# Sums of batch 2 for a layer norm: five GpSimd additions, tile by tile, in place of four VectorE reductions

## The chip, the cores and the metric

The kernel runs on one core of a Trainium2 chip. The metric is the device time of one execution in microseconds (us). The core has five engines that run side by side, each through its own queue in order: TensorE (PE in the rows; PEld is its weight load), VectorE (DVE), ScalarE (ACT), GpSimd (POOL) and SyncE (SP, which here only issues DMAs). They meet through semaphores: an instruction that needs another engine's result waits, and everything behind it on its own engine waits too.

## The reference

Attention with normed queries and keys, then two MLPs, all in float32. The part around the change is the mean over features in the first MLP's layer norm, which is taken over the attention's output.

```python
q_n, k_n = rmsnorm(q, g_q), rmsnorm(k, g_k)
scores = scale * np.matmul(q_n, k_n.transpose(0, 1, 3, 2))    # 4 batches, 12 heads, 448 x 448
attn = np.exp(scores - np.max(scores, axis=-1, keepdims=True))
attn = attn / (np.sum(attn, axis=-1, keepdims=True) + 1e-09)
x = np.matmul(attn, v)                                        # then to (4, 448, 768)
...
mu = np.mean(x, axis=-1, keepdims=True)
var = np.mean((x - mu) ** 2, axis=-1, keepdims=True)
xn = (x - mu) / np.sqrt(var + 1e-06) * g_ln
x = x + np.maximum(xn @ w_ch1, 0.0) @ w_ch2
...
u = x + (x.transpose(0, 2, 1) @ U @ V).transpose(0, 2, 1)
out = u + np.maximum(u @ w_ch1, 0.0) @ w_ch2
```

## The kernel before

Each batch's activations `x[b]` lie in SBUF as six tiles of 128 features by 448 tokens (`x[b][:, k, :]`, KD = 6). The kernel has two stages: attention (to about 339 us in the profile) and the MLPs, whose order is set by a planner of its own.

In the attention stage the function `attention` runs 48 heads in a software pipeline. Its loop calls generators, one step of each per quarter of a head: `sc` makes scores (`ps`, L491 and L492) and exponentials (`p`, ACT, L494), `mx` makes scores the other way round (`pm`, L455) and their maxima on VectorE (`m`, L456), `t1` and `t2` transpose (`pk`, `pq`, `pt`), `pv` multiplies by the values (`po`, L509), and `norm` copies the result out of PSUM (`u`, L523) and sends it to `x[b]` and, for the sums of the exponentials, to DRAM.

A list `ln` holds side work that advances by one step of its first generator in each quarter of a head. When the twelve heads of batch 2 are through, it holds in this order: `scale` (reads the sums back, inverts them, spreads them over the partitions as tiles `r`, and multiplies the six tiles of `x[2]` by them on VectorE, L564); `ln_stats(2)`; `early`, which narrows the first MLP weights from float64 (integer joins on VectorE, `join` L83 and `sign` L87) and splits them into a high and a low part (a cast on ScalarE, L945, a subtraction on GpSimd, L946, tiles `w0` to `w5`); the first steps of `scale` for batch 3; and `late`, more weights.

`ln_stats` makes the sums over features in two steps. First four reductions on VectorE, one for each 112 tokens, add the six tiles into one 128x448 tile `xs` (L163). Then a matmul with a matrix of 1/768 adds over the partitions (L169, into the PSUM tile `ln`), and ScalarE copies the mean to `mu` (L172). Six subtractions on GpSimd (L184), squares on ScalarE (L187), sums on VectorE (L181) and a second matmul (L192) make the variance.

A scheduler puts the attention stage's instructions in order on each engine, by its own estimates; those wrapped in `pin`, the norm's matmuls and the scalings among them, keep the program's order. The reductions and the GpSimd operations are not pinned.

Of the kernel before, what the change touches and what calls it, by code (L numbers as in the profile page):

```python
# [8 lines left out]
F32 = mybir.dt.float32  # L9
# [5 lines left out]
ALU = mybir.AluOpType  # L15
AX = mybir.AxisListType

B, H, S, D = 4, 12, 448, 64
P = 128
# [28 lines left out]
def build(tc, qkv, gg, g_ln, w1a, w2a, w1b, w2b, u_in, v_in, out):  # L48
    nc = tc.nc
    V, A, PL, PE = nc.vector, nc.scalar, nc.gpsimd, nc.tensor  # L50
    with ExitStack() as es:
# [96 lines left out]
            by(V.scalar_tensor_tensor(t, t, -0.5, a, ALU.mult, ALU.mult))  # L148
            by(V.scalar_tensor_tensor(y if to is None else to, t, 1.5, y, ALU.add, ALU.mult))

        lns, side = {}, {}

        def ln_stats(b, pool=None):
            def lt(n, pool=None):
                if pool:
                    return pool.tile([P, S], F32, tag="lx", name=f"ln{b}_{n}", bufs=4)
                return lpool.tile([P, S], F32, tag="lt", name=f"ln{b}_{n}")

            lag = 2 if pool else 1
            xs = lt("xs")  # L160
            for c in range(NC):
                cs = slice(c * CP, (c + 1) * CP)
                V.tensor_reduce(xs[:, cs], x[b][:, :, cs].rearrange("p k n -> p n k"), AX.X, ALU.add)  # L163
                yield
            yield
            if pool:
                yield
            pm = side["ln"] if pool else bank("mu")
            pin(PE.matmul(pm[:, :S], ones_m, xs, start=True, stop=True))  # L169
            yield  # L170
            mu = lt("mu")
            pin(A.copy(mu, pm[:, :S]))  # L172
            yield
            acc = lt("acc")
            run = pm[:, :S] if pool else acc
            sqs = {}
            gap = 2 * lag
            for n in range(KD + gap):
                k = n - gap
                if k > 0:  # L180
                    pin(V.tensor_tensor(acc if k == KD - 1 else run, run, sqs[k], ALU.add))  # L181
                if n < KD:
                    sqs[n] = acc if n == 0 else lt(f"sq{n}", pool if n != KD - 2 else None)
                    PL.tensor_tensor(sqs[n], x[b][:, n, :], mu, ALU.subtract)  # L184
                k = n - lag
                if 0 <= k < KD:
                    pin(A.activation(sqs[k] if k else run, sqs[k], AF.Square))  # L187
                yield
            for _ in range(lag):
                yield  # L190
            va = pm if pool else bank("var")
            pin(PE.matmul(va[:, :S], ones_m, acc, start=True, stop=True))  # L192
            yield
            y, a, t = acc, va[:, :S], xs if pool else lt("nt")
            pin(V.tensor_scalar(a, a, EPS, None, ALU.add))
            yield
            pin(A.activation(y, a, AF.Ln))
            pin(A.activation(y, y, AF.Exp, scale=-0.5))
            yield
            rsqrt_newton(y, a, t, a if pool and b < 2 else y)  # L200
            yield
            lns[b] = (mu, a if pool and b < 2 else y)
# [23 lines left out]
        def attention(ap, ep, ep2, early, late):  # L226
# [300 lines left out]
                q.dma_start(st["sum", b][h:h + 1, :], u[D:D + 1, :])  # L527
                yield

            def scale(b, q, h0, h1, pool=None):  # L530

                def fold(d):
                    return d[h0:h1].rearrange("h s -> (h s)").rearrange("(p n) -> p n", p=P)

                n = (h1 - h0) * S // P
                s = lpool.tile([P, n], F32, tag="sc", name=f"ss{b}_{h0}", bufs=2)
                q.dma_start(s, fold(st["sum", b]))
                yield
                y = lpool.tile([P, n], F32, tag="sc", name=f"sy{b}_{h0}", bufs=2)
                yield  # L540
                pin(A.activation(y, s, AF.Ln, bias=tiny))
                pin(A.activation(y, y, AF.Exp, scale=-1.0))
                yield
                pin(V.scalar_tensor_tensor(s, s, 1e-9, y, ALU.add, ALU.mult))
                V.tensor_tensor(s, s, y, ALU.mult)
                V.scalar_tensor_tensor(y, y, 2.0, s, ALU.mult, ALU.subtract)
                yield
                d = dpool.tile([H, S], F32, tag="rs", name=f"rs{b}_{h0}")
                q.dma_start(fold(d), y)
                yield  # L550
                ks = range(h0 // 2, h1 // 2)
                rs = {}
                lag = 3 if pool else 2
                for n in range(len(ks) + lag):
                    if n < len(ks):
                        k = ks[n]
                        rs[k] = (f32(pool)[:, n, :] if pool else
                                 lpool.tile([P, S], F32, tag="lt", name=f"r{b}_{k}"))
                        for j in range(2):
                            q.dma_start(rs[k][j * D:(j + 1) * D, :],  # L560
                                        d[2 * k + j:2 * k + j + 1, :].to_broadcast([D, S]))
                    if n >= lag:
                        k = ks[n - lag]
                        pin(V.tensor_tensor(x[b][:, k, :], x[b][:, k, :], rs[k], ALU.mult))  # L564
                    yield
# [9 lines left out]
            for i in range(-3 - T1, NH + 2):  # L575
                def ok(n):
                    return 0 <= n < NH
                if i == -3 - T1:
                    start = first_two()
                    next(start)  # L580
                elif i == -1 - T1:
                    bg.append(start)
                elif i in (1 - T1, 3 - T1):
                    bg.append(pre((i + T1 + 3) // 2))
                if i > 3 - T1 and (i + T1) % 2 == 0 and (i + T1 + 4) // 2 < NP:
                    bg.append(pre((i + T1 + 4) // 2))
                if i % 2:
                    if 0 <= (i + 1) // 2 < NP:
                        bg.append(pre_v((i + 1) // 2))
                tasks = [f(n) for f, n in (ORD(i)) if ok(n)]  # L590
                if i == 4:
                    ln.append(load_uv())
                if i - 2 in (H, 2 * H, 3 * H):
                    b = (i - 2) // H - 1
                    ln.append(scale(b, nc.sync, 0, H, xl[b] if b < 2 else None))
                if i - 2 in (H, 2 * H):
                    ln.append(ln_stats(b, ap))
                    ln.append(ln_apply(b, ap))
                if i - 2 == 3 * H:
                    ln.append(ln_stats(2, ap))  # L600
                    most = scale(B - 1, nc.sync, 0, HL)
                    ln += [early, islice(most, 5), late]
                for c in range(NC):
                    bg = [t for t in bg if next(t, 1) is None]
                    tasks = [t for t in tasks if next(t, 1) is None]
                    if ln and next(ln[0], 1) == 1:
                        ln.pop(0)
                assert not tasks and not bg or i < NH + 1
# [906 lines left out]
```

## Time and profile before

| what | value |
|---|---|
| median of three runs | 1677.04 us (1676.89 to 1685.16) |
| the profiled execution | 1676.77 us |
| its span, from first to last instruction | 1674.5 us |
| around the span | 2.27 us |
| PE busy | 1659.7 us, 99% |
| DVE busy | 1218.4 us, 73% |
| POOL busy | 1087.7 us, 65% |
| ACT busy | 1003.2 us, 60% |

The span is what the profile's rows cover; the execution's own time holds 2.27 us more. Busy shares are means over both stages. The rows below give start times from the span's start, so that an instruction can be found in all views by its start.

### The profile page before, as it was taken

To read this page: it belongs to the slowest core of one execution; us is meant where nothing else is said; L and a number is where in the kernel's file an instruction comes from. 1 tells how busy PE (TensorE), PEld (TensorE's weight loads), DVE (VectorE), ACT (ScalarE), POOL (GpSimd) and SP (SyncE) were. 2 spreads that over 40 slices of the span, in tenths; PEclk is the share of its full clock that TensorE was granted. 3 is DMA by queue.
4 is the path that set the end of the run, shared out by engine and by line. 5 is a ranking of instruction groups with operands and counts; after the bars stand their busy time and mean duration, and the time that the engine had idled before them with its cause. 6 is when DMAs were issued, how large, how long until landed. Compare 5 with 4: busy or idle time off the path is not lost.

```text
span 1674.5 us, 24807 instructions
## 1 busy us (share of the span) xinstructions
PE 1659.7 (99%) x8251; PEld 1442.0 (86%) x8251; DVE 1218.4 (73%) x1941; ACT 1003.2 (60%) x2105; POOL 1087.7 (65%) x963
## 2 busy tenths in 40 slices
PE   8999999999999999999999999999999999999999
PEld 6676666589999999999999999999999999999998
DVE  6878787879887887866767686667667854565665
ACT  6888888767878866554544455444445534454541
POOL 5788767449767787755555587555555655776752
PEclk8999999999999999999999999999999999999999
DMA  3444445776755566544444427565657463443432
GB/s 97 117 100 116 120 117 138 200 223 199 243 173 178 180 212 200 187 141 134 152 133 158 162 83 257 187 219 179 224 192 246 169 207 116 149 151 123 149 125 76
DMA packets 134432, 273.42 MB, mean 163 GB/s; under 512 B 37280, under 2 KB 57664, under 8 KB 134304
## 3 DMA queue, kind: packets, MB, share of 16 engines
q1 hardware_dynamic: 112252, 265.24, 49.8%
q10 hardware_dynamic: 22052, 6.59, 1.7%
q8 instruction: 66, 1.08, 0.3%
q14 instruction: 62, 0.51, 0.1%
HBM read 178.80 MB, written 81.96 MB: 156 GB/s over the span
## 4 chain that ended last, share of the span: by engine, by line
PE 89%; DMA 3%; DVE 3%; issue 2%; ACT 1%; POOL 1%; SPq 0%; POOLq 0%; DVEq 0%; ACTq 0%
PE bank L1120 34%; PE bank L1298 32%; PE bank L1242 6%; PE po L509 4%; PE b L1120 2%; PE b L1242 2%; PE ps L491 2%; PE pm L455 2%; PE ps L492 1%; DVE m L456 1%; DMA raw<-in_qkv 1%; PE t L987 1%; PE xt L977 1%; PE pk L434 1%; PE pq L442 1%
## 5 line engine op out<-in xcount | busy, mean ns | idle before, releaser
L1298 PE MATMUL bank<-h,w 128*128 128x448 f32 x2655 | 586.4, 366 | 0.3 <-DVE h L1112 0.3
L1298 PEld LDWEIGHTS bank<-h,w 128*128 128x128 f32 x2655 | 497.2, 188 | 40.0 <-DVE h L1112 0.6
L1309 DVE TENSOR_TENSOR x<-x,bank 128x448 f32<-128x448 f32 x450 | 275.9, 616 | 192.9 <-PE bank L1298 188.1
L1120 PE MATMUL bank<-xh,w 128*128 128x448 f32 x1158 | 330.4, 367 | 0.0
L794 POOL TENSOR_TENSOR w<-wf,w 128x384 fp32r<-128x384 f32 x201 | 222.6, 1118 | 131.6 <-ACT w L793 131.5
L794 POOL TENSOR_TENSOR w<-s,w 128x384 fp32r<-128x384 f32 x151 | 173.8, 1154 | 155.3 <-ACT w L793 149.9
L1120 PE MATMUL bank<-T,w 128*128 128x448 f32 x1134 | 251.9, 367 | 0.0
L1120 PEld LDWEIGHTS bank<-xh,w 128*128 128x128 f32 x1158 | 216.9, 188 | 18.1 <-issue 0.8
L1120 PEld LDWEIGHTS bank<-T,w 128*128 128x128 f32 x1134 | 211.9, 188 | 16.8
L1120 PE MATMUL bank<-xl,w 128*128 128x448 f32 x579 | 211.7, 366 | 0.0
L793 ACT CAST w<-s 128x384 fp32r<-128x384 f32 x151 | 77.0, 515 | 178.5 <-PE bank L1120 166.0
L793 ACT CAST w<-wf 128x384 fp32r<-128x384 f32 x201 | 101.5, 514 | 101.2 <-PE bank L1120 82.6
L456 DVE TENSOR_REDUCE m<-pm 112x1 f32<-112x448 f32 x192 | 118.5, 619 | 46.4 <-PE pm L455 45.7
L509 PE MATMUL po<-p,vf 112*66 112x448 f32 x328 | 149.8, 539 | 0.1
L83 DVE SCALAR_TENSOR_TENSOR wf<-wf,raw 128x384 uint32<-128x384 uint32 x180 | 134.2, 752 | 10.4 <-ACT raw L71 3.8
L794 POOL TENSOR_TENSOR w<-raw,w 128x384 fp32r<-128x384 f32 x72 | 81.2, 1145 | 57.2 <-ACT w L793 57.1
L1120 PEld LDWEIGHTS bank<-xl,w 128*128 128x128 f32 x579 | 108.8, 188 | 8.7
L79 ACT ACTIVATE wf<-raw 128x384 f32<-128x384 f32 x180 | 99.3, 553 | 20.7 <-DMA raw<-in_w2a 9.5
L494 ACT ACTIVATE p<-ps 112x448 f32<-112x448 f32 x192 | 104.6, 547 | 6.2 <-PE ps L492 3.5
L1112 DVE SCALAR_TENSOR_TENSOR h<-tm,h 128x448 fp32r<-128x448 f32 x103 | 102.2, 992 | 2.8 <-ACT h L1111 2.1
L71 ACT ACTIVATE raw<-raw 128x384 uint32<-128x384 uint8 x180 | 99.9, 558 | 0.0
L1161 DVE TENSOR_TENSOR tm<-tm,bank 128x448 f32<-128x448 f32 x102 | 63.0, 617 | 47.7 <-PE bank L1120 46.8
(283 smaller groups left out, 2989.5 us busy)
## 6 DMA issues: line engine op xcount, KB each, us to landing
wd<-wf SPq DMA_DIRECT2D x94, 384.0 KB
ws<-w SPq DMA_DIRECT2D x84, 384.0 KB
w<-ws SPq DMA_DIRECT2D x84, 384.0 KB
wf<-wd SPq DMA_DIRECT2D x51, 384.0 KB
raw<-wd SPq DMA_DIRECT2D x48, 384.0 KB
raw<-in_w1b SPq DMA_DIRECT2D x48, 384.0 KB
raw<-in_w2b SPq DMA_DIRECT2D x48, 384.0 KB
raw<-in_w2a SPq DMA_DIRECT2D x44, 384.0 KB
```

The costliest lines, as they stand in the source:

```text
L71: A.activation(r[:, :, 0], r.bitcast(U8).rearrange("p n (t q) -> p n t q", t=2)[:, :, 0, 3], AF.Copy, scale=1.0 / 32, bias=-31.0 / 64)
L83: V.scalar_tensor_tensor(f, f, 3, r[:, :, 0], ALU.logical_shift_left, ALU.bitwise_or)
L456: V.tensor_reduce(m[:, c:c + 1], pm[:CP, :S], AX.X, ALU.max)
L494: A.activation(p, pb[:CP, :S], AF.Exp)
L509: PE.matmul(po[:QW, :S], vf[:, j, c, :], ps[c], start=(i == 0), stop=(i == NC - 1))
L793: job(A, 520, lambda: A.copy(form(key)[0], src()), ins, ("hi",) + key, [key])
L794: job(PL, 1100, lambda: PL.tensor_tensor(form(key)[1], src(), f32(form(key)[0]), ALU.subtract), [("hi",) + key], key, rel=rel)
L1112: soon(V, 700, lambda: V.scalar_tensor_tensor(at(*key)[:, 1], src(), 0.0, f32(at(*key)[:, 0]), ALU.max, ALU.subtract), [("hh",) + key], ke ...
L1120: PE.matmul(out[:, :S], wt[:, k, :], xt[:, k, :], start=(first and n == 0), stop=(last and n == 8), skip_group_check=True)
L1242: PE.matmul(at(*to)[:, :S], wt[:, e, :], xt, start=(m in "13" and n == 0), stop=(n == 2), skip_group_check=True)
L1298: PE.matmul(at(*key)[:, :S], wt[:, e % 3, :], t, start=(n == 0), stop=(n == 3 * G - 1))
L1309: V.tensor_tensor(x[b][:, e, :], x[b][:, e, :], at(*key)[:, :S], ALU.add)
```

## The change

For batch 2 alone, `scale` gets `add=True`: after the sixth load of `r` it takes the tile `xs` and adds the scaled tiles into it on GpSimd, five additions of 128x448 (the first joins tiles 0 and 1). `scale` then has one step more. `ln_stats(2)` finds `xs` in `sums` and leaves out the four reductions together with their six steps, so that it begins with the mean's matmul. All work behind it in the list `ln` thus comes five steps sooner. Batches 0, 1 and 3 keep the reductions.

```diff
--- before.py
+++ after.py
@@ -148,7 +148,7 @@
             by(V.scalar_tensor_tensor(t, t, -0.5, a, ALU.mult, ALU.mult))
             by(V.scalar_tensor_tensor(y if to is None else to, t, 1.5, y, ALU.add, ALU.mult))
 
-        lns, side = {}, {}
+        lns, side, sums = {}, {}, {}
 
         def ln_stats(b, pool=None):
             def lt(n, pool=None):
@@ -157,14 +157,17 @@
                 return lpool.tile([P, S], F32, tag="lt", name=f"ln{b}_{n}")
 
             lag = 2 if pool else 1
-            xs = lt("xs")
-            for c in range(NC):
-                cs = slice(c * CP, (c + 1) * CP)
-                V.tensor_reduce(xs[:, cs], x[b][:, :, cs].rearrange("p k n -> p n k"), AX.X, ALU.add)
-                yield
-            yield
-            if pool:
-                yield
+            if b in sums:
+                xs = sums.pop(b)
+            else:
+                xs = lt("xs")
+                for c in range(NC):
+                    cs = slice(c * CP, (c + 1) * CP)
+                    V.tensor_reduce(xs[:, cs], x[b][:, :, cs].rearrange("p k n -> p n k"), AX.X, ALU.add)
+                    yield
+                yield
+                if pool:
+                    yield
             pm = side["ln"] if pool else bank("mu")
             pin(PE.matmul(pm[:, :S], ones_m, xs, start=True, stop=True))
             yield
@@ -527,7 +530,7 @@
                 q.dma_start(st["sum", b][h:h + 1, :], u[D:D + 1, :])
                 yield
 
-            def scale(b, q, h0, h1, pool=None):
+            def scale(b, q, h0, h1, pool=None, add=False):
 
                 def fold(d):
                     return d[h0:h1].rearrange("h s -> (h s)").rearrange("(p n) -> p n", p=P)
@@ -551,7 +554,7 @@
                 ks = range(h0 // 2, h1 // 2)
                 rs = {}
                 lag = 3 if pool else 2
-                for n in range(len(ks) + lag):
+                for n in range(len(ks) + lag + add):
                     if n < len(ks):
                         k = ks[n]
                         rs[k] = (f32(pool)[:, n, :] if pool else
@@ -559,7 +562,12 @@
                         for j in range(2):
                             q.dma_start(rs[k][j * D:(j + 1) * D, :],
                                         d[2 * k + j:2 * k + j + 1, :].to_broadcast([D, S]))
-                    if n >= lag:
+                    if add and n >= len(ks) - 1:
+                        if n == len(ks) - 1:
+                            sums[b] = xs = lpool.tile([P, S], F32, tag="lt", name=f"ln{b}_xs")
+                        for k in (1, 2) if n == len(ks) - 1 else (n - lag - 1,):
+                            PL.tensor_tensor(xs, x[b][:, 0, :] if k == 1 else xs, x[b][:, k, :], ALU.add)
+                    if lag <= n < len(ks) + lag:
                         k = ks[n - lag]
                         pin(V.tensor_tensor(x[b][:, k, :], x[b][:, k, :], rs[k], ALU.mult))
                     yield
@@ -592,7 +600,7 @@
                     ln.append(load_uv())
                 if i - 2 in (H, 2 * H, 3 * H):
                     b = (i - 2) // H - 1
-                    ln.append(scale(b, nc.sync, 0, H, xl[b] if b < 2 else None))
+                    ln.append(scale(b, nc.sync, 0, H, xl[b] if b < 2 else None, b == 2))
                 if i - 2 in (H, 2 * H):
                     ln.append(ln_stats(b, ap))
                     ln.append(ln_apply(b, ap))
```

The lines of the changed file are numbered 3 higher after `ln_stats` and 8 higher after `scale`. In the rows of the two orders that follow, a name is tile, its running number, and a number of the build after the last underscore.

On PE, near the end of head 44 (scores `ps552` to `ps555`), the order before has the mean's matmul `ln1<-ln2_xs` here:

```order
L442 MATMUL pq554_4441<-identr_309,qd23_4244 128x112 x4
L169 MATMUL ln1_305<-ln2_xs_4346,ones_m_75 128x448
L491 MATMUL ps555_4449<-bq_44_4223,a1_44_4177 112x448
L492 MATMUL ps555_4449<-t2_44_4362,a22_364 112x448
L455 MATMUL pm556_4454<-a1_46_4340,bq_46_4379 112x448
L509 MATMUL po547_4403<-p43_3_4385,vf1_354 66x448
```

In the changed kernel it stands in head 43's last half (scores `ps537` to `ps543`), behind the transposes `pt2539`:

```order
L512 MATMUL po535_4339<-p42_1_4282,vf1_354 66x448
L472 MATMUL pt2539_4361<-identr_309,ql1_368 66x112 x4
L172 MATMUL ln1_305<-ln2_xs_4273,ones_m_75 128x448
L494 MATMUL ps540_4369<-bq_43_4137,a1_43_4090 112x448
L495 MATMUL ps540_4369<-t2_43_4293,a21_362 112x448
L458 MATMUL pm541_4374<-a1_45_4264,bq_45_4312 112x448
```

The matmul has moved 24 rows up on PE, ahead of `ps540`. The variance's matmul moves too, from the values' products of the last head (`po578`) to just ahead of the first scores of that head (`ps573`).

On POOL, after the last low part of the queries (`ql2`), before:

```order
L317 TENSOR_TENSOR ql2_370<-raw23_0_3848,qd23_4244 112x8x64
L946 TENSOR_TENSOR w0_277<-wf0_4630,w0_277 128x384
L946 TENSOR_TENSOR w1_278<-wf0_4630,w1_278 128x384
L946 TENSOR_TENSOR w2_279<-wf1_4648,w2_279 128x384
L946 TENSOR_TENSOR w3_280<-wf1_4648,w3_280 128x384
L184 TENSOR_TENSOR ln2_acc_4479<-x2_84,ln2_mu_4459 128x448
```

In the changed kernel:

```order
L320 TENSOR_TENSOR ql2_370<-raw23_0_3848,qd23_4244 112x8x64
L569 TENSOR_TENSOR ln2_xs_4273<-x2_84 128x448
L954 TENSOR_TENSOR w0_277<-wf0_4625,w0_277 128x384
L569 TENSOR_TENSOR ln2_xs_4273<-ln2_xs_4273,x2_84 128x448 x3
L954 TENSOR_TENSOR w1_278<-wf0_4625,w1_278 128x384
L569 TENSOR_TENSOR ln2_xs_4273<-ln2_xs_4273,x2_84 128x448
L954 TENSOR_TENSOR w2_279<-wf1_4649,w2_279 128x384
L187 TENSOR_TENSOR ln2_acc_4397<-x2_84,ln2_mu_4385 128x448
```

The five additions stand between the same neighbours, mixed with the first three weight subtractions; the next one of these, `w3`, now comes behind the norm's subtractions.

On DVE, from the sixth scaling of batch 2 on, before:

```order
L564 TENSOR_TENSOR x2_84<-x2_84,r2_5_4270 128x448
L87 SCALAR_TENSOR_TENSOR wf1_4648<-wr10_4626,wf1_4648 128x384
L163 TENSOR_REDUCE ln2_xs_4346<-x2_84 128x112
L456 TENSOR_REDUCE m45_4329<-pm538_4353 112x1
L163 TENSOR_REDUCE ln2_xs_4346<-x2_84 128x112
L456 TENSOR_REDUCE m45_4329<-pm541_4370 112x1
L163 TENSOR_REDUCE ln2_xs_4346<-x2_84 128x112
L456 TENSOR_REDUCE m45_4329<-pm544_4387 112x1
L163 TENSOR_REDUCE ln2_xs_4346<-x2_84 128x112
```

In the changed kernel:

```order
L572 TENSOR_TENSOR x2_84<-x2_84,r2_5_4270 128x448
L87 SCALAR_TENSOR_TENSOR wf1_4649<-wr10_4620,wf1_4649 128x384
L459 TENSOR_REDUCE m45_4335<-pm538_4357 112x1
L83 SCALAR_TENSOR_TENSOR wf1_4649<-wf1_4649,wr11_4622 128x384
L459 TENSOR_REDUCE m45_4335<-pm541_4374 112x1
L87 SCALAR_TENSOR_TENSOR wf1_4649<-wr11_4622,wf1_4649 128x384
L459 TENSOR_REDUCE m45_4335<-pm544_4392 112x1
```

The four reductions are gone and the weights' joins have moved up into their places; the scalings stand where they did.

## Rows read from the trace of the kernel before

**Rows 1.** The page: busy us (share of the span) and instructions.

```profile
PE 1659.7 (99%) x8251; PEld 1442.0 (86%) x8251; DVE 1218.4 (73%) x1941; ACT 1003.2 (60%) x2105; POOL 1087.7 (65%) x963
```

**Rows 2.** Windows: stretch, its us, busy PE PEld DVE ACT POOL, PEclk, DMA, GB/s.

```profile
307.12:318.69 11.57, 11.16 (x52) 5.90 (x50) 11.57 (x18) 9.73 (x24) 3.00 (x3) 1.00 0.74 212
318.69:338.67 19.98, 19.33 (x72) 10.06 (x71) 15.63 (x31) 16.11 (x39) 9.52 (x8) 1.00 0.73 213
338.67:1674.50 1335.83, 1332.09 (x6607) 1230.22 (x6605) 952.95 (x1432) 728.88 (x1463) 851.95 (x749) 1.00 0.53 173
```

**Rows 3.** Timeline of PE: start us, us, line, operation, out<-in, shapes.

```profile
289.29 0.72 PE L491 MATMUL ps<-bq,a 128*112 128x448 f32 x1
...
292.93 0.41 PE L491 MATMUL ps<-bq,a 128*112 128x448 f32 x1
...
294.63 0.43 PE L491 MATMUL ps<-bq,a 128*112 128x448 f32 x1
...
295.71 0.72 PE L491 MATMUL ps<-bq,a 128*112 128x448 f32 x1
...
306.56 0.73 PE L469 MATMUL pt<-identr,ql 112*66 112x112 f32 x4
...
307.12 0.41 PE L491 MATMUL ps<-bq,a 128*112 128x448 f32 x1
...
316.85 0.99 PE L169 MATMUL ln<-ln_xs,ones_m 128*128 128x448 f32 x2
...
318.69 0.72 PE L491 MATMUL ps<-bq,a 128*112 128x448 f32 x1
```

**Rows 4.** Timeline of DVE, 301 to 316 us.

```profile
301.47 1.63 DVE L87 SCALAR_TENSOR_TENSOR wf<-wr,wf 128x384 uint32<-128x384 uint32 x1
...
303.56 0.61 DVE L564 TENSOR_TENSOR x<-x,r 128x448 f32<-128x448 f32 x1
...
305.03 0.61 DVE L456 TENSOR_REDUCE m<-pm 112x1 f32<-112x448 f32 x1
...
306.62 0.61 DVE L564 TENSOR_TENSOR x<-x,r 128x448 f32<-128x448 f32 x1
...
307.62 1.36 DVE L163 TENSOR_REDUCE ln_xs<-x 128x112 f32<-128x672 f32 x1
...
313.00 1.34 DVE L163 TENSOR_REDUCE ln_xs<-x 128x112 f32<-128x672 f32 x1
...
315.30 0.56 DVE L83 SCALAR_TENSOR_TENSOR wf<-wf,wr 128x384 uint32<-128x384 uint32 x1
```

**Rows 5.** Timeline of POOL, then the norm's subtractions: count, ns min/median/max, first and last start.

```profile
301.02 1.67 POOL L317 TENSOR_TENSOR ql<-raw,qd 112x512 fp32r<-112x512 f32 x1
...
303.73 2.25 POOL L946 TENSOR_TENSOR w<-wf,w 128x384 fp32r<-128x384 f32 x1 [1.04 <-ACT w L945]
...
305.94 2.63 POOL L946 TENSOR_TENSOR w<-wf,w 128x384 fp32r<-128x384 f32 x1
...
310.48 1.01 POOL L946 TENSOR_TENSOR w<-wf,w 128x384 fp32r<-128x384 f32 x1 [1.91 <-ACT w L945]
...
L184 POOL TENSOR_TENSOR ln_sq<-x,ln_mu x20: 1126/1144/1566, 151.4 to 547.3; 128x448 f32<-128x448 f32 x20
```

**Rows 6.** Timeline of PE and of ACT, 329 to 331 us.

```profile
329.35 0.71 PE L491 MATMUL ps<-bq,a 128*112 128x448 f32 x1
...
330.71 0.46 PE L492 MATMUL ps<-t,a 66*112 66x448 f32 x1 [0.65 <-ACT t L471]
...
329.49 0.32 ACT L541 ACTIVATE sy<-ss,tiny 128x28 f32<-128x28 f32 x1 [0.58 <-DMA ss<-sum]
```

**Rows 7.** Windows near the start, columns as in the second group.

```profile
5.08:15.32 10.24, 8.63 (x73) 7.88 (x72) 8.35 (x18) 7.19 (x18) 3.84 (x3) 1.00 0.68 163
15.32:25.56 10.24, 7.07 (x31) 5.61 (x32) 7.79 (x16) 6.59 (x17) 4.97 (x5) 0.50 0.14 34
25.56:35.80 10.24, 9.31 (x48) 5.98 (x47) 7.04 (x16) 9.11 (x22) 6.60 (x7) 1.00 0.34 91
```

## The prediction

> **What bounds the kernel now.** I read the split of busy time first: TensorE (PE) is busy in 99% of the span, the next engine in 73% [rows 1]. So only what stops PE can be won, and whatever newly stops PE is paid in full. I then went to the stretch that the change touches, the end of the attention stage. Across 307.12:318.69 VectorE (DVE) is busy for all 11.57 us and GpSimd (POOL) for 3.00 [rows 2]: there DVE is the crowded engine and POOL has room. After 338.67 PE is busy 1332.09 of 1335.83 us [rows 2], so nothing there will give back a delay made here.
>
> On PE, heads come in regular steps. An undisturbed head takes 295.71 − 289.29 = 6.42 us [rows 3]. The reader is to see what the crowded stretch loses against that. From the step at 307.12 to the head at 318.69 PE takes 11.57 us. The same steps undisturbed are 295.71 − 292.93 = 2.78, plus one head of 6.42, plus the mean's matmul `ln<-ln_xs`: the step that holds it lasts 318.69 − 316.85 = 1.84 against 295.71 − 294.63 = 1.08, so it costs 0.76 [rows 3]. That makes 9.96; 1.61 us are lost. A further 0.65 is lost at 330.71, where PE waits for a ScalarE (ACT) copy that is queued just behind a tile waiting for a DMA (329.49) [rows 6]. These 2.26 us are what less work on DVE can win at most.
>
> **What goes.** Four reductions of some 1.3 us, from 307.62 to 314.34, leave DVE [rows 4]. They read one SBUF input. Nothing else goes.
>
> **What is added.** Five additions of 128x448 on POOL, which has no row of this shape with the accumulator, but has the same operation on the same tile: the subtractions of `ln_sq`, 1.14 us in the median, 1.13 to 1.57 [rows 5]. I take 1.14 each, 5.7 together. POOL's room of 8 us in the stretch would hide that, if nothing had to wait for it.
>
> **What moves.** The order shows that the generator, which now yields less often, puts the mean's matmul 24 rows earlier on PE: from between `pq554` and `ps555` (316.85) to between `pt2539` and `ps540`. Those two start at 306.56 and 307.12 [rows 3]. PE executes in order, so at 307.12 it now stands until the fifth addition is done, and behind it stand all scores, and with them DVE's maxima and ACT's exponentials. The fifth addition cannot begin before the sixth scaling ends, 307.23 (306.62 plus 0.61) [rows 4], so some stall is certain. The question is how long the additions take.
>
> **The price of POOL beside DVE.** The same POOL subtraction of 128x384 takes 1.01 us at 310.48, between two of the reductions, but 2.25 at 303.73 and 2.63 at 305.94, beside scalings and the integer joins L83 and L87 [rows 5]. The first ends 0.95 us after DVE turned to the PSUM maximum at 305.03 [rows 4, 5]. The reverse also shows: L87 started at 301.47 and took 1.63, to 303.10, where a join alone takes 0.56 (315.30), while the POOL subtraction of 301.02 ran until 302.69 [rows 4, 5]. So here the two exclude each other when DVE's instruction reads two SBUF tiles, and reductions disturb nobody.
>
> The Trainium skill, GPSIMD Engine Reference, section 1 (Specifications), says that GpSimd shares its SBUF interfaces with VectorE, with contention when a DVE instruction reads two SBUF inputs or runs in a two-port mode. The trace agrees, 1.01 us beside reductions and 2.25 beside scalings. By this rule the change takes away instructions that never contended and adds some that do.
>
> **The chain, step by step.** POOL is free at 302.69, but the waiting L87 goes first, to 303.10.
> - Addition 1: 303.10 to 304.24. The scaling of 303.56 waits for it, then runs with the two joins behind it, in before 303.56 to 305.03, 1.47 [rows 4]: to 305.71.
> - The subtraction `w0`, 1.01: to 306.72. Addition 2: to 307.86. DVE meanwhile does the 1.59 between 305.03 and 306.62 and then waits with the last scaling.
> - Scaling and join, 1.00 (306.62 to 307.62 [rows 4]): to 308.86. Addition 3: to 310.00.
> - The join L83 that now follows at once, 0.56 [rows 4]: to 310.56. After it DVE's queue holds the maximum of `pm541`, which PE issues only behind its stall, so DVE contends no more.
> - Addition 4 to 311.70, `w1` to 312.71, addition 5 to 313.85.
>
> PE stands from 307.12 to 313.85, 6.7 us. If DVE lets POOL in at every chance, the seven POOL instructions alone are 5 × 1.14 + 2 × 1.01 = 7.7, from 303.10 to 310.8: a stall of 3.7. If each took the 2.63 of the worst row, they would end at 321.5: 14.4. The chain is near the first end because DVE runs dry; I take 6.5.
>
> **What is given back.** During the stall DVE clears its backlog, without the reductions it stays clear, and the sum of the heads reaches its DMA earlier. I count 2.0 of the 2.26 us. The variance's matmul also moves forward, to the first scores of the last head, 329.35 in before [rows 6]. From 307.12 that is 22.2 us less the 0.76 and the 1.61 of above, some 20, and six subtractions of 1.14 with their squares and sums have to fit in; I count no wait. Scaling, DMA issues and the MLP stage keep their order but for a load or two; nothing.
>
> **TensorE's clock.** After 5.08:15.32, with PE busy for 8.63 of 10.24 us, the granted clock fell to 0.50 (1.2 GHz) for the whole of 15.32:25.56, then went back to 1.00 (2.4 GHz) [rows 7]. A stall of 6.5 us is more idle time in a row than anything in that stretch, so I expect such a fall. Half the clock for 10.24 us costs 5.1 at most, and less for the part that lies in the stall itself or on work that is not bound by the clock: 2.5 to 5.1, I take 3.5.
>
> **Sum.** 6.5 − 2.0 + 3.5 = 8.0 us on the profiled execution's 1676.77, which is 0.27 below the median of 1677.04: 1684.8 us, +0.5%. About 0.5%, 8.4 us, is what a measurement of this kernel can tell from no change; the forecast lies just inside it.
>
> **The rivals.**
> - *Stall without the fall of the clock:* the trace also shows lesser idle times, like the 0.65 at 330.71, with the clock left at 1.00 throughout [rows 2, 6]. Then 6.5 − 2.0 = 4.5: 1681.3.
> - *A longer stall:* the additions contend like the rows of 2.25 and 2.63 throughout. For it: in the second of these the time that DVE left free, before 306.62 and after 307.62, adds to 1.6, not 1.0 [rows 4, 5]. Against it: DVE's queue runs dry at `pm541`. Halfway to the bound, a stall of 10.4: 10.4 − 2.3 + 3.5 = 11.6, 1688.4.
> - *The other side, a small gain:* POOL gets through early, and PE arrives late because DVE's maxima are delayed by addition 1. It decides where the stall is under 2.3 us. Even with the additions 1 to 4 done in time, the fifth ends at 307.23 + 1.14 = 308.37, a stall of 1.25 against 2.26 won: −1.0, 1675.8. Faster by over 0.5% has no mechanism here, since all that can be won is 2.3 us.
> - *The change does little:* the stall is mostly given back because other waits of the stage would have come anyway: +2, 1679.
>
> **How the numbers follow.** Stall and fall 0.60 (own range 1682.3 to 1687.3), stall alone 0.17, longer stall 0.10, small gain 0.07, little 0.06. The range leaves out the gain, part of the little and the end of the longer stall: 1679.5 to 1688.5. Slower by over 0.5% (above 1685.4): the longer stall, and half of the first case: 0.40. Faster: 0.03. The rest, 0.57, is within 0.5%.
>
> **What would show it.** Right: one idle gap of PE before the matmul of `ln2_xs`, about 4 to 8 us, ended by POOL's addition; five additions at some 1.1 to 2 us, the joins beside them stretched; no `ln_xs` reduction of batch 2 on DVE; no gap at the later ACT copy; a stretch of granted clock 0.50 near 313 to 323. Wrong: if PE shows no gap of over 2 us there, the chain failed; if the gap is there and the clock stays at 1.00, that term; if the total moves by more than gap, clock and 2.3 us explain, something in the MLP stage that I count as nothing.

## The result, and the profile after

| kernel | median, us | lowest to highest | executions | ratio to before, 95% interval |
|---|---|---|---|---|
| before | 1677.55 | 1676.89 to 1685.16 | 7 | |
| changed | 1688.14 | 1684.29 to 1694.04 | 7 | 1.0057 [1.0034, 1.008] |

The change makes the kernel 0.57% slower. The predicted 1684.8 us is 3.3 too low; it lay just within 0.5% of before, the result lies just beyond, with an interval that reaches to both sides of 0.5%. It is inside the predicted range, close to its upper end. Two later sets of the same kernel were slower still: 1.0099 [1.0083, 1.0115] and 1.0081 [1.0058, 1.0103]. Over all 17 executions the median is 1691.45, above the range's end of 1688.5, so it is in part luck that the first seven fell inside.

The profiled execution took 1694.04 us, with a span of 1692.2: 17.7 more than before. The page's split of busy time answers to [rows 1]:

```profile
PE 1671.1 (99%) x8251; PEld 1444.9 (85%) x8251; DVE 1219.1 (72%) x1937; ACT 1003.7 (59%) x2105; POOL 1086.8 (64%) x968
```

DVE has four instructions less and POOL five more, as the diff says. Of PE's 17.7 us, 11.4 are more busy time, so it was not only waiting but also slower. Its waits from 300 to 355 us:

```profile
engine line waited for: us in total, times, longest us
PE pm L458 <- DVE m L459: 3.9, 1, 3.9
PE bank L1128 <- DVE u L526: 2.4, 1, 2.4
PE pm L458 <- ACT bq L448: 0.7, 1, 0.7
PE ln L172 <- POOL ln_xs L569: 0.5, 1, 0.5
```

The mean's matmul (`ln`, now L172), which was to stand for 6.5 us, waits 0.5. The large wait is that of a maximum's matmul `pm` for its PSUM buffer, which VectorE's maximum of an earlier one (L459) sets free. The timeline of DVE shows how late that maximum was:

```profile
303.55 0.61 DVE L459 TENSOR_REDUCE m<-pm 112x1 f32<-112x448 f32 x1
304.08 3.08 DVE L572 TENSOR_TENSOR x<-x,r 128x448 f32<-128x448 f32 x1
307.09 1.48 DVE L87 SCALAR_TENSOR_TENSOR wf<-wr,wf 128x384 uint32<-128x384 uint32 x1
308.49 1.48 DVE L83 SCALAR_TENSOR_TENSOR wf<-wf,wr 128x384 uint32<-128x384 uint32 x1
309.89 0.61 DVE L459 TENSOR_REDUCE m<-pm 112x1 f32<-112x448 f32 x1
```

And the timeline of POOL why:

```profile
303.17 1.45 POOL L569 TENSOR_TENSOR ln_xs<-x 128x448 f32<-128x448 f32 x1
304.59 0.99 POOL L954 TENSOR_TENSOR w<-wf,w 128x384 fp32r<-128x384 f32 x1
305.54 1.14 POOL L569 TENSOR_TENSOR ln_xs<-ln_xs,x 128x448 f32<-128x448 f32 x1
...
306.76 1.39 POOL L569 TENSOR_TENSOR ln_xs<-ln_xs,x 128x448 f32<-128x448 f32 x1
...
308.23 1.33 POOL L569 TENSOR_TENSOR ln_xs<-ln_xs,x 128x448 f32<-128x448 f32 x1
```

The fifth scaling (L572) took 0.61 us in [rows 4] and 3.08 here. It came while addition 1 ran (303.17 to 304.62), and stayed outside through `w0` and addition 2 as well: these three follow each other with no time between (the next starts at 304.59 and 305.54, before the one ahead has ended). It ends at 307.16, so with its 0.61 it began about 306.55, as addition 2 ended (306.68); 0.08 us lie between that and addition 3. Then each join (0.56 alone, [rows 4]) took 1.48 beside one addition, and the maximum that frees the PSUM buffer began at 309.89 and not at 305.03 [rows 4].

The windows of PE's stretches answer to [rows 2]; columns as there:

```profile
307.12:318.69 11.57, 7.66 (x19) 4.08 (x20) 7.62 (x12) 4.48 (x11) 5.95 (x5) 0.57 0.51 164
318.69:338.67 19.98, 19.98 (x86) 11.59 (x86) 16.48 (x30) 17.97 (x44) 8.91 (x7) 0.99 0.58 156
349.65:353.06 3.41, 3.41 (x11) 3.02 (x10) 0.62 (x1) 1.75 (x4) 2.77 (x3) 0.50 0.84 276
```

PE made 19 matmuls where it made 52. The granted clock was 0.50 (1.2 GHz) from 308.69 to 318.93, and once more for 3.41 us at the start of the MLPs. PE's timeline answers to [rows 3]:

```profile
310.56 0.72 PE L458 MATMUL pm<-a,bq 128*112 128x448 f32 x1 [3.92 <-DVE m L459]
...
313.62 1.86 PE L172 MATMUL ln<-ln_xs,ones_m 128*128 128x448 f32 x2 [0.48 <-POOL ln_xs L569]
314.60 1.25 PE L494 MATMUL ps<-bq,a 128*112 128x448 f32 x1
...
319.09 0.36 PE L458 MATMUL pm<-a,bq 128*112 128x448 f32 x1
...
326.11 0.72 PE L494 MATMUL ps<-bq,a 128*112 128x448 f32 x1
...
348.24 0.68 PE L1128 MATMUL bank<-xh,w 128*128 128x448 f32 x2 [2.41 <-DVE u L526]
```

The scores that began at 307.12, the head at 318.69 and the first MLP matmul at 338.67 [rows 2, 3] now begin 7.48, 7.42 and 9.57 us later. About 0.5 of each is older than the change: PE was that late at 300 us. Between the last two stands the second wait, before the MLP's first matmul. The chain of work from 343 to 348 us (start, us, what) leads there:

```profile
343.39 0.64 DVE ln_xs L147
...
344.05 0.06 DVE ln_xs L148
...
344.59 0.15 DVE u L526
...
345.12 0.62 DVE ln_acc L149
...
345.80 0.67 ACTq L530
...
346.52 0.55 ACT wr L71
...
347.09 0.06 DVE wf L83
...
347.57 0.62 DVE u L526
...
348.24 4.05 PE bank L1128 x13
```

L147 to L149 are the end of the variance's inverse root, which now comes before the copies of the last heads. The copy `u` (L526) that ends a head stands behind the first two of them on DVE. ACT waits for it with the issue of that head's DMA (L529, L530), and cannot convert the next weight (L71) till 346.52; a join (L83) on DVE waits for that weight, and behind the join stands the last copy `u`, which frees the PSUM bank that the MLP wants.

### The profile page after: what moved, and what is told of

Its sections match the earlier page's. It is cut to its first block, busy times and chain, and to the rows that moved or that the text cites. A ratio compares the mean times of both kernels' runs of the same rounds, so it can differ in the third digit from the quotient of the medians.

```text
span 1692.2 us, 24803 instructions
## 1 busy us (share of the span) xinstructions
PE 1671.1 (99%) x8251; PEld 1444.9 (85%) x8251; DVE 1219.1 (72%) x1937; ACT 1003.7 (59%) x2105; POOL 1086.8 (64%) x968
## 4 chain that ended last, share of the span: by engine, by line
PE 90%; DVE 3%; ACT 2%; DMA 2%; POOL 2%; issue 2%; ACTq 0%; SPq 0%; POOLq 0%; DVEq 0%
PE bank L1128 35%; PE bank L1306 33%; PE bank L1250 6%; PE po L512 4%; PE b L1128 2%; PE b L1250 2%; PE ps L494 2%; PE pm L458 2%; PE ps L495 1%; DVE m L459 1%; PE t L995 1%; PE xt L985 1%; ACT p L497 1%; PE pq L445 1%; PE pk L437 0%
## 5 line engine op out<-in xcount | busy, mean ns | idle before, releaser
L459 DVE TENSOR_REDUCE m<-pm 112x1 f32<-112x448 f32 x192 | 118.3, 618 | 47.6 <-PE pm L458 47.0
L83 DVE SCALAR_TENSOR_TENSOR wf<-wf,raw 128x384 uint32<-128x384 uint32 x180 | 133.9, 750 | 8.1 <-ACT raw L71 3.9
L71 ACT ACTIVATE raw<-raw 128x384 uint32<-128x384 uint8 x180 | 100.2, 559 | 0.0
```

The lines of the kernel that those rows point to most:

```text
L71: A.activation(r[:, :, 0], r.bitcast(U8).rearrange("p n (t q) -> p n t q", t=2)[:, :, 0, 3], AF.Copy, scale=1.0 / 32, bias=-31.0 / 64)
L83: V.scalar_tensor_tensor(f, f, 3, r[:, :, 0], ALU.logical_shift_left, ALU.bitwise_or)
L459: V.tensor_reduce(m[:, c:c + 1], pm[:CP, :S], AX.X, ALU.max)
```

## The experiments

Each kernel was timed beside runs of the kernel before on the same chip. Late by means here: start of a matmul less the start of the same one in the trace of before.

**again, again2: the changed kernel itself**, for its spread.

> The changed kernel itself, once more. Its first trace is later than before by 6.7 us at the end of attention, by 11.0 us at 350 us, and by 17 at 730: from 353 to 733 us its matmuls follow each other at 206.6 ns in place of 202.7, with the granted clock at 1.00. Theory: the stall near 306 to 314 and the first fall of the clock belong to the change and come back; the slower pitch (some 6 us) belongs to a single execution and is not there in each, so that the time is near the middle of the earlier runs, 1684 to 1690. Rival: the pitch comes with the change, and this trace has it too from the start of the MLPs on.

> The changed kernel once more, for the spread of its executions, which was 1684 to 1695. Theory A (two ways of running the MLP stage's first 380 us, with a pitch of 202.7 or of 206.7 ns from one matmul to the next at the full granted clock, decided at the short fall of the clock at its start): the times fall into two groups about 6 us apart, near 1687 and 1693, and the profiled one shows the pitch of its group. Rival B (the spread is from several small waits): no groups, and the profiled one's distance from 1687 lies in gaps.

Measured: 1693.35 us (1687.4 to 1694.58, 4 executions) and 1694.41 (1684.9 to 1695.62, 6). The trace of `again` repeats the gap of 3.94, the wait of 0.5 at the mean's matmul, the second gap (2.8) and both stretches of clock 0.50 (308.43 to 318.67, 349.39 to 352.80). But its execution took 1687.4, against 1694.04 of the first. The difference lies in the MLPs. The window of 360 to 700 us in the first trace of the changed kernel:

```profile
360.00:700.00 340.00, 340.00 (x1644) 308.23 (x1643) 280.15 (x396) 254.69 (x489) 241.89 (x203) 1.00 0.61 191
```

and in that of `again`:

```profile
360.00:700.00 340.00, 340.00 (x1676) 314.52 (x1675) 285.23 (x402) 255.33 (x492) 248.91 (x208) 1.00 0.62 193
```

With PE busy throughout and the granted clock at 1.00, the one makes 1644 matmuls, the other 1676: 340/1644 = 206.8 ns each in place of 202.9. Before made 1672, `again2` 1643. Until 734 us that adds 6.3 us to PE's lateness, then the pace is the old one. So the theory of `again` held for its trace, but its median lies above the 1684 to 1690 that it gave. Of the 17 executions 7 lie at or under 1688.16, 7 at or over 1694.04, and 3 between: nearly the two groups of theory A of `again2`. What starts the slow pace stays open; of the traces here, three with the short fall of the clock at the MLP's start have it (the first of the changed kernel, `again2` and `after_scale`) and two don't (`again`, `late_tail`), and none of those without that fall. Nor is it shown to come with the change: three of the 62 executions of the kernel before took 1684.3 to 1685.2 us, over 7 more than its medians, and no trace here is of one of them.

**late_mean: five empty steps ahead of the mean's matmul**, so that it and the variance stand where they stood before; the additions stay.

```diff
                 xs = sums.pop(b)
+                for _ in range(5):
+                    yield
```

> The additions stay on GpSimd where they are, but the mean's matmul and all that follows it go back to their old places by five empty steps. Theory A (port): the gap of 3.9 us on TensorE before a maximum's matmul at 310.6 comes from the additions keeping VectorE off its SBUF tiles (the scaling took 3.08 us, two joins 1.48 each), so it stays, the clock falls with it, and the time is 1681 to 1687 us. Theory B (early matmul): TensorE stands because the mean's matmul comes before the additions are done; then no gap over 1 us is left near 300 to 320, the clock stays at 1.00 and the time is 1675 to 1679 us.

Measured: 1680.95 us, ratio 1.0016 [1.0006, 1.0027]. On DVE's timeline the scaling of 303.25 took 3.08. PE's waits:

```profile
PE pm L460 <- DVE m L461: 3.9, 1, 3.9
```

The shut-out scaling, its gap and a stretch of 6.82 us at clock 0.50 are all there with the mean's matmul out of the way, and the second gap is gone. So the large stall comes from the additions, not from the mean's place, and costs about 4 us together with its fall of the clock; the rest of the loss comes from the early mean and variance. That is theory A, with a time 0.05 us under its 1681 to 1687.

**dve_adds: the five additions on VectorE**, the mean early as in the change.

```diff
-                            PL.tensor_tensor(xs, x[b][:, 0, :] if k == 1 else xs, x[b][:, k, :], ALU.add)
+                            V.tensor_tensor(xs, x[b][:, 0, :] if k == 1 else xs, x[b][:, k, :], ALU.add)
```

> The five additions on VectorE at the places where they are made, the mean's matmul early as in the change. Theory A (port): nothing shuts VectorE out any more; no gap over 1.5 us near 300 to 320, clock at 1.00, and VectorE has 5 times 0.62 = 3.1 us in place of 5.4 of reductions: 1675 to 1679 us at the end, but for what the earlier tail costs at the start of the MLPs (up to 4 us). Theory B (early matmul): TensorE still waits at the mean's matmul for the fifth addition, 2 to 5 us, with a fall of the clock: 1680 to 1686 us.

Measured: 1679.82 us, ratio 1.0014 [1.0005, 1.0023]. On DVE the additions take 0.61 us, but the one at 307.81 took 1.42, beside the weight subtractions of POOL, and PE lost 1.72 behind a late maximum at 309.81. A fall of the clock to 0.50 came with it. The gap:

```profile
309.81 1.76 PE L512 MATMUL po<-p,vf 112*66 112x448 f32 x2 [1.72 <-DVE m L459]
```

and the window (columns as in [rows 2]):

```profile
309.05:315.88 6.83, 6.07 (x18) 3.55 (x19) 6.57 (x13) 1.81 (x4) 0.00 (x0) 0.50 0.76 257
```

Shutting out works in this direction too, at a smaller price. Neither theory held as it stood: theory A had no such gap and no fall, theory B a wait at the mean's matmul, which did not come. The mean's matmul was put elsewhere by the scheduler here (at 316.82), so this kernel does not separate the two effects cleanly.

**after_scale: the same five additions in another order**, so that the first has to wait for the fifth scaling.

```diff
-                        for k in (1, 2) if n == len(ks) - 1 else (n - lag - 1,):
-                            PL.tensor_tensor(xs, x[b][:, 0, :] if k == 1 else xs, x[b][:, k, :], ALU.add)
+                        for k in () if n < len(ks) else {6: (), 7: (4, 2, 1, 0), 8: (5,)}[n]:
+                            PL.tensor_tensor(xs, x[b][:, 3, :] if k == 4 else xs, x[b][:, k, :], ALU.add)
```

> The changed kernel with the five additions in another order (tile 4 with tile 3 first, then tiles 2, 1, 0 and 5), so that GpSimd's first addition has to wait for the fifth scaling, the one that took 3.08 us in the changed kernel. The order of TensorE, VectorE and ScalarE stays that of the changed kernel; on GpSimd two subtractions of the weights now stand ahead of the additions. Theory A (VectorE's scaling is shut out by the additions in front of it, its maxima come late behind it, and TensorE stands for a PSUM buffer): the scaling takes about 0.6 us, the gap of 3.9 us before the maximum's matmul shrinks under 1 us; the five additions then come late, from about 309 to 316, and TensorE stands at the mean's matmul for 6 to 9 us, as the prediction had it; total 1688 to 1694. Rival B (the gap before the maximum's matmul is of another cause, the order or ScalarE): it stays near 3.9 us, with the wait at the mean's matmul added to it; total over 1694.

Measured: 1689.13 us, ratio 1.008 [1.0065, 1.0095]. The fifth scaling on DVE, at 304.52, took 0.61, and the joins behind it 0.54 each. POOL beside them:

```profile
304.68 2.25 POOL L954 TENSOR_TENSOR w<-wf,w 128x384 fp32r<-128x384 f32 x1 [1.04 <-ACT w L953]
306.89 2.76 POOL L569 TENSOR_TENSOR ln_xs<-x 128x448 f32<-128x448 f32 x1
```

and PE's waits:

```profile
PE ln L172 <- POOL ln_xs L569: 7.3, 1, 7.3
PE bank L1128 <- DVE u L526: 2.2, 1, 2.2
```

As theory A expected: with DVE inside first, it is POOL that waits, the gap at `pm` is gone, and PE stands 7.3 us at the mean's matmul; the granted clock was 0.50 from 311.95 to 318.78. This is the stall that the prediction described, at the place that it named, with its 6.5; the change's own order of additions led to the other one.

**late_tail: five empty steps behind the norm's statistics**, a try at the second gap.

```diff
+            if early_mean:
+                for _ in range(5):
+                    yield
             lns[b] = (mu, a if pool and b < 2 else y)
```

> The change, with five empty steps behind the norm's statistics, so that the weights' work that follows them keeps its old distance from the end of attention. Theory: the second gap of TensorE, 2.4 us before the first matmul of the MLPs, comes from the tail's new order (the last copy of a head's result stands behind a join that waits for a weight's load); then it goes, with the short second fall of the clock, and the time is 3 to 5 us under the changed kernel's: 1681 to 1685 us. Rival: the second gap comes from the lateness itself; it stays, and the time is the changed kernel's, 1686 to 1690 us.

Measured: 1686.84 us, ratio 1.0059 [1.0047, 1.0072], as the rival had it. The second gap stays:

```profile
PE bank L1133 <- DVE u L531: 2.5, 1, 2.5
```

The place of the work that follows the statistics is not its cause.

**late_var: the same empty steps ahead of the variance's matmul.**

```diff
+            if early_mean:
+                for _ in range(5):
+                    yield
             va = pm if pool else bank("var")
```

> The changed kernel with five empty steps of the generator between the norm's sum of squares and the matmul for its variance, so that the mean stays early and the variance's matmul and its chain on ScalarE and VectorE go back to where they stood before the change, behind the attention stage's last matmuls. Theory A (the early variance's two VectorE instructions delay the copy of the last heads' sums, and ScalarE's issue of its transfer holds up the weight joins behind it, so that the MLP's first matmul waits for a PSUM bank): the second gap, 2.4 to 2.8 us near 348 us, goes, and the short fall of the clock behind it; the first gap stays at 3.9; total 4 to 5 us under the changed kernel's, 1681 to 1685. Rival B (the second gap follows from the whole program being some 9 us late against its loads and weights, whatever stands there): the gap stays, total within 1 us of the changed kernel's 1688 to 1693.

Measured: 1684.88 us (1681.36 to 1689.94), ratio 1.0051 [1.0036, 1.0067]. PE's waits:

```profile
PE pm L463 <- DVE m L464: 3.9, 1, 3.9
PE bank L1133 <- DVE u L531: 0.7, 1, 0.7
```

With the variance late, the second gap falls from 2.4–2.8 to 0.7, and the short fall of the clock is gone. Theory A holds but for a rest of 0.7. In this trace PE was 2.7 us late ahead of the stretch already, from several small waits between 12 and 300 us that no edit touches; from there to the end it lost 6.3, against 10.0 in `again`. The early variance alone does not make the gap: in `dve_adds` and `busy_gap` its matmul stands early too, and PE has no wait before the MLP. There ScalarE's conversion of the last weight (L71, at 343.53 in `dve_adds`) comes ahead of the issue of the head's DMA (L529, 343.99); in the changed kernel it comes behind it (346.52 and 345.23). So, as far as these traces show, it takes both, the early variance and this order on ScalarE.

**busy_gap: five unused matmuls in the gap**, the change otherwise as it is.

```diff
+                    if n == 45 and c == 1:
+                        for _ in range(5):
+                            pin(PE.matmul(side["ln"][:, :S], ones_m, x[0][:, 0, :], start=True, stop=True))
                     PE.matmul(pm[:CP, :S], bq[:, c * CP:(c + 1) * CP], a1, start=True, stop=True)
```

> The changed kernel with five extra matmuls, 128x128 by 128x448 in fp32, whose result nothing uses, put on TensorE just ahead of the maximum's matmul before which it stood for 3.9 us. They fill the gap with work and leave the wait what it is. Theory A (the fall of the granted clock to 0.50 for 10.24 us follows from the idle time, and costs about 3.5 us on top of the gap): no stretch of 0.50 near 309 to 319, TensorE's lag against the kernel before is some 5 us behind the stretch in place of 9.4, total 3 to 4 us under the changed kernel's unless the second gap takes another shape. Rival B (the clock's fall costs little, since VectorE and ScalarE bound the stretch anyway): the clock stays at 1.00, but the lag behind the stretch stays at 8 to 9.5 us, total within 1 us of the changed kernel's. Rival C (the fall has another cause): the clock falls all the same.

Measured: 1687.9 us, ratio 1.0058 [1.0046, 1.007]. The window of the stretch:

```profile
307.00:320.60 13.60, 10.10 (x36) 4.91 (x35) 9.53 (x14) 6.00 (x14) 7.56 (x7) 1.00 0.58 187
```

and PE's timeline in it:

```profile
311.12 0.46 PE L461 MATMUL pm<-a,bq 128*112 128x448 f32 x1 [0.19 <-DVE m L462]
...
314.18 1.02 PE L172 MATMUL ln<-ln_xs,ones_m 128*128 128x448 f32 x2 [1.63 <-POOL ln_xs L572]
...
317.16 0.36 PE L461 MATMUL pm<-a,bq 128*112 128x448 f32 x1
...
319.96 0.46 PE L497 MATMUL ps<-bq,a 128*112 128x448 f32 x1 [1.68 <-ACT t L477]
```

The clock stayed at 1.00 in the stretch: the idle time had caused its fall. From the `pm` behind the gap to the `pm` at 317.16 PE took 6.04 us, 4.41 without the wait at the mean's matmul; the same matmuls took 319.09 − 310.56 = 8.53 in the changed kernel, 8.05 without its wait of 0.48. So the fall costs PE 3.6 us of slower matmuls. The stretch as a whole is shorter by 2.5 only (8.53 less 6.04), since PE without the fall waits 1.63 for POOL in place of 0.48. Theory A is right in the cause and in the price of the slower matmuls; what could be won here is less than its 3 to 4. The total does not show it, because the scheduler also put ScalarE's queue in another order: the transposed tile `t` now stands behind a weight that waits 1.67 us for its DMA, and PE waits 1.68 and 1.06 more, with a fall of the clock from 320.60 to 327.43. So the total tells nothing here, the stretch up to 317.16 does.

**dve_end: the four reductions replaced by five additions on VectorE at the same steps**, in the kernel before.

```diff
+                if b == 2:
+                    for k in (1, 2) if c == 0 else (c + 2,):
+                        V.tensor_tensor(xs, x[b][:, 0, :] if k == 1 else xs, x[b][:, k, :], ALU.add)
+                    yield
+                    continue
```

> The kernel before with the four reductions replaced by five additions of whole tiles on VectorE, at the reductions' steps, the mean's matmul where it stood before. Nothing is added on GpSimd. Theory A (whatever two-input instructions GpSimd and VectorE run at the same time shut each other out): the additions, of two SBUF tiles each, take about 0.6 us where GpSimd is idle and 1 to 2.5 where its weight subtractions run; some 1 us less VectorE work than four reductions of 1.3, TensorE's idle 1.6 us in the stretch shrink a little, total 1675 to 1679, no fall of the clock. Rival B (each addition of two inputs is held up by GpSimd's subtractions beside it, and the maxima with it): a gap of 1 to 3 us before a maximum's or another matmul and a fall of the clock, total 1679 to 1684, as with the additions on VectorE and an early mean.

Measured: 1676.15 us, ratio 0.9998 [0.9989, 1.0007]; four additions at 0.61 us and one at 0.89, no fall of the clock. VectorE is relieved of 2 us in the stretch (9.45 busy in 307.12:318.69 against 11.57 [rows 2]), and the time stays.

**pool_late: after_scale and late_mean together**: additions on GpSimd that start behind the fifth scaling, mean and variance at their old places.

> The five additions on GpSimd, begun only after the fifth scaling (order of the additions as in after_scale), and five empty steps ahead of the mean's matmul, so that it and all behind it on TensorE stand where they stood in the kernel before. Theory A (the change costs its time by two things alone, the scaling that is shut out and the mean and variance that come early): neither is left, no gap over 1 us before a maximum's matmul or the mean's, no fall of the clock in the stretch, and VectorE has four reductions less, so at most the 2.3 us of idle time of the kernel before are won: total 1674 to 1677.5. Rival B (GpSimd's additions hold up VectorE wherever they are put, since its joins have two inputs too): the joins take over 1 us each, a maximum comes late, and a gap of 1 to 4 us with a fall of the clock follows: total 1679 to 1684.

Measured: 1675.31 us (1673.87 to 1677.15), ratio 0.9986 [0.9976, 0.9997]. The window that answers to the first of [rows 2]:

```profile
307.12:318.69 11.57, 10.89 (x50) 6.17 (x49) 8.62 (x14) 9.58 (x24) 9.67 (x8) 1.00 0.76 244
```

PE's waits from 300 to 355 us:

```profile
PE pm L460 <- ACT bq L450: 0.7, 1, 0.7
PE pt L474 <- ACT ql L466: 0.7, 1, 0.7
```

POOL is busy for 9.67 us where it was for 3.00, DVE for 8.62 where it was for 11.57. No large gap, no fall of the clock: moving the sums to GpSimd is worth 0.14% once it keeps clear of DVE's scalings and the norm's matmuls stay late. It is the only version whose interval lies below the kernel before.

The totals also hold the small waits ahead of the stretch and the pace of the MLPs. By how much PE's lateness grows between 300 and 345 us of before, matmul by matmul, leaves both out: 10.4 us in the changed kernel, 10.6 in `again`, 11.0 in `after_scale`, 10.2 in `late_tail`, 9.7 in `busy_gap`, 6.6 in `late_var`, 4.3 in `late_mean`, 2.7 in `dve_adds`, 0.3 in `dve_end`; in `pool_late` it shrinks by 1.2.

## Why the prediction was nearly right, and where not

The direction, the stretch and the fall of the clock were right; one step failed, one term was missing, and their errors go against each other: 6.1 us in place of 8.0 up to the end of attention, then 4.3 in place of nothing. That the sum came near is in part luck. By its own sign ("if PE shows no gap of over 2 us there, the chain failed") the chain failed: ahead of the matmul of `ln2_xs` PE waits 0.5 us. The move beyond what its terms explain came, as it said, from something that it counted as nothing.

- **The stall (6.5 predicted).** The step that failed is "The scaling of 303.56 waits for it, then runs with the two joins behind it". It waited not for one GpSimd instruction but for all that stood back to back, 3.08 us, and then each join waited for one more. So PE stood at `pm`, 3.9 us, and at the mean's matmul only 0.5: 4.4 in place of 6.5. The shape of the prediction does exist, as `after_scale` shows with 7.3 at the mean's matmul; which of the two comes depends on who is inside first. The Trainium skill, SBUF — State Buffer, section "SBUF: two separate sides", says that the shared ports are locked for a whole instruction and that the one who comes second waits fully; the trace agrees (3.08 for 0.61), and adds that the waiting one may miss several turns in a row.
- **The clock (3.5).** The fall came at 308.69 to 318.93, near the foretold 313 to 323. `busy_gap` gives its price as 3.6 of slower matmuls; without the fall PE would have waited 1.1 longer for POOL, so 2.5 of it is net.
- **Given back (−2.0).** The gap of 0.65 before the ACT copy [rows 6] is gone. From the scores at 307.12 to the head at 318.69 PE took as long as before (7.48 and 7.42 late) although 4.3 us of it ran at 0.50: without the mean's matmul (0.76) and the 1.61 of lost time in between, there was room for that. What is left over in the changed kernel, 4.4 + 3.6 less the 6.1 below, is 1.9; `pool_late`, where neither stall is left, puts the whole of it at 1.3 us by its medians and 1.2 by its trace.
- **The end of the attention stage.** At the last value matmuls (336.76 in before, 343.41 after) PE was 6.65 us late, some 6.1 of it from the change, where 8.0 was the sum.
- **"Scaling, DMA issues and the MLP stage ... nothing".** This is the term that was missing. The variance's end came ahead of the last heads' copies, through VectorE, ScalarE's queue and a PSUM bank to 2.4 us of waiting, and a short fall of the clock behind it: 11.0 late at 354 us, +4.3. With the 6.1 that makes 10.4; `again`, which lacks the slow pace, lost 10.0 from 300 us to the end. With the variance late 0.7 is left of the wait of 2.4 to 2.8 (`late_var`), with the mean late too nothing (`late_mean`). The prediction counted how long the variance's matmul would wait for its inputs, but not who waits behind what it lets start.
- **The slow pace in the MLPs**, 6.3 us in the profiled execution, stood in no row of before. It makes the difference between the executions near 1687 and those near 1694.
- **The rivals.** The stall without a fall of the clock (1681.3) did not occur, nor the small gain; the "longer stall" names the right cause (GpSimd and VectorE hold each other up more than once) and its 1688.4 is next to the median, but by luck: PE stood less long than it says, and the rest came at the start of the MLPs.

What stays open: the cause of the slow pace, the rest of 0.7 us in `late_var`, and why the same gap of 3.9 us was followed by 10.24 us of lower clock in some traces and by 6.83 in others.

## What to carry to other kernels

Before an operation goes to GpSimd, list VectorE's two-input SBUF instructions around its new place and what waits behind each of them: here a run of three GpSimd instructions without pauses held up the first of them for the whole run, and the PSUM buffer that a maximum a few instructions further on sets free paid for it. When work at the end of a stage comes sooner, follow what it now stands ahead of in every queue up to the next stage's first instruction. And read a stall's price together with the clock's: here 4.4 us of waiting came with 3.6 more of slower matmuls.

## What was not expected of the hardware

- VectorE's scaling of 0.61 us took 3.08 to 3.09 in all seven traces in which GpSimd's first addition ran ahead of it, past two further GpSimd instructions, and by its end it got in where 0.08 us lay between two of them.
- The matmuls of the MLP ran at 206.8 ns in place of 202.9 for some 380 us, at a granted clock of 1.00, in some executions and not in others of the same kernel.
- A gap of 2.4 us at the MLP's start was followed by a granted clock of 0.50 for only 3.41 us, against 10.24 behind the gap of 3.9; in `late_mean`, `late_tail` and `late_var` the gap of 3.9 was followed by 6.82 or 6.83, and in `dve_adds` a gap of 1.72 by 6.83.
